# Softmax of later batches transposed by VectorE blocks and a quarter exchange, one TensorE burst per head pair, W_in in 256-column pieces, a new order

## The chip, the cores and the metric

The kernel runs on one core of a Trainium2 chip. The time is that of one execution on the device, in microseconds (us); several runs are taken and their median is given. One further execution was recorded by the hardware profiler, and all rows below are from it.

## What is computed

Eight batches of eight heads, 576 positions, head size 64. The first four heads attend to a local window of 32 positions, the other four to all earlier positions with the same remainder modulo 32. The result, 4608 tokens by 512, goes through a two-layer network with a gate.

```python
scores = scale * np.matmul(q, k.transpose(0, 1, 3, 2))
mask_local = (rel >= 0) & (rel < stride)
mask_strided = (rel >= 0) & (pos[None, :] % stride == pos[:, None] % stride)
...
attn = np.exp(scores - max) / (sum + 1e-09)
x = np.matmul(attn, v)                      # (4608, 512)
h = x @ w_in                                # 512 -> 2048
g = h * erf(softplus(h))
out = g @ w_out                             # 2048 -> 512
```

The weights arrive as 64-bit floats and everything else as 32-bit floats.

## The kernel before

**Precision.** The large products are computed in three terms: each operand is split into a rounded high part and a remainder (`hi`, `lo`), and hi*hi, hi*lo and lo*hi are added up. The 64-bit weights are loaded as pairs of 32-bit words, and VectorE puts a 32-bit float together from their bits (`bits0`, `bits1`, `bits2`, lines 612, 619 and 625), ScalarE takes the high part (line 630), VectorE the remainder (line 633). There are 16 such pieces: eight of W_in (256 rows by 512 columns) and eight of W_out (256 rows by 512 columns), 1 MB each as they are loaded.

**Attention.** `heads` treats one pair of heads of one batch, 32 pairs in all. For masks as sparse as these only small blocks of the scores are computed, 32 or 64 queries by 64 keys, and stacked on the partitions. The steps: load q and k, then v (lines 363, 366); `scores` on TensorE (line 377, 80 small matmuls for a local pair, 48 for a strided one); on VectorE `mask`, `maxi`, `less` (lines 407, 413, 425); `exp` on ScalarE (line 434); `total` and `invert` on VectorE (458, 467, 468); `norm` on GpSimd (475); `turn` on TensorE, six transposes of 128 by 128 into PSUM (484); `fetch`, a copy to SBUF by ScalarE (490); `av` on TensorE (503, 72 or 44 small matmuls); and the split of the result into `xhi` and `xlo` (522, 527). The eight pairs of batches 0 and 1 use other banks and buffers (`PAIRS`); their softmax is partly done by ScalarE alone (449), their mask is added by TensorE (390), and some of their loads lie in buffers that later hold weights. The 24 later pairs use one region `ps` of two PSUM banks, first for the scores, then for the transposed weights of attention, then for the result.

**The network.** A chunk is 512 tokens of a batch; the last 64 tokens of each batch are put by in DRAM (808) and form a ninth chunk of 512 (814). `ftile` treats 128 of the 2048 hidden columns of one chunk, 144 times in all, numbered k: 12 matmuls `mm1` into a bank `h` (line 661, 4 blocks by 3 terms), `softplus` on ScalarE from `h` (666), `gate` (erf, 669), `prod` on VectorE (672, reads `h` again), the two parts `ghi` (675, ScalarE) and `glo` (678, VectorE), and four groups of three matmuls `mm2` into the banks `o0` to `o3` (708). After the last hidden column of a segment the four banks are copied out (729, 727) and stored (732) or added to what is stored (742). Two consecutive ftiles share their activation tables: softplus twice, erf twice. `SEGS` is the order in which chunks 0 and 1 take hidden columns, in segments of 4 or 8 of the 16 blocks, since W_in and W_out are still arriving; chunks 2 to 8 take all 16 at once.

**Order.** `Plan` holds every step with its engine, a duration and a key, and writes down one fixed order for each engine before the kernel is built: at each moment the step with the lowest key among those that could start. `KP`, `KW`, `KI` and `FT` are the keys. Instructions then run on each engine in this order and wait only for semaphores. PSUM has eight banks: `h` two, `ps` two, `o0` to `o3` one each. While TensorE has nothing else in the first stage, `warm` matmuls on constants are put in (851).

Of the kernel before, what the change touches and what calls it, by code (L numbers as in the profile page):

```python
# [31 lines left out]
FT = (150.531, 835.645, -384.189, -1053.44, -681.063, 898.966)  # L32
KI = -3209.9
KW = (
    (101.599, 202.151, -535.174, 604.781, 1212.9, 836.522, 1608.98, 546.558),
    (361.736, 4.05449, 627.481, 738.31, 1066.48, 1640.11, 660.969, 255.795),
)
KP = (
    (95.8804, -1256.4, 246.738, 210.68, 388.629, 267.383, -232.968),
    (89.0881, -257.397, 181.554, 106.998, -422.473, 270.564, -29.6347),  # L40
    (39.7309, 257.811, 444.048, 228.671, -192.767, 289.834, -736.755),
    (-746.766, -31.9878, 336.097, -221.418, 982.13, -1173.26, 113.144),
    (96.5419, -322.814, 849.876, 940.658, 220.734, 127.612, 110.26),
    (448.329, 235.899, 647.027, -140.7, -533.241, 575.841, -534.673),
    (140.403, 484.365, 38.2845, 536.795, -628.605, -59.6376, 5.88654),
    (427.907, 538.096, 156.093, -147.993, -594.918, -613.259, -1.35456),
    (1021.68, 1227.51, 317.55, 1305, 395.946, 827.8, 422.359),
    (-428.223, -259.323, 505.653, -625.444, -366.792, -81.8236, -265.431),
    (22.7174, 1266.92, 869.655, 629.419, 756.918, 1001.81, 769.097),
    (-341.314, 324.887, 467.314, -208.725, 85.0777, -457.75, 85.4845),  # L50
    (-189.06, 539.726, -625.551, -295.899, -556.918, -965.588, -631.652),
    (1609.6, 847.563, 528.29, 890.427, 1474.46, 704.536, 355.295),
    (-514.483, -397.182, -437.853, 681.903, 612.634, 326.529, 1144.86),
    (741.667, 393.174, -749.662, -494.021, 28.442, 173.094, 247.963),
    (797.248, 187.08, 566.957, 523.594, 793.895, 602, 318.908),
    (366.017, -645.078, -99.5954, 310.3, -964.063, 384.338, 209.526),
    (631.465, 206.076, 1156.93, 1362.17, 893.28, 848.748, -88.8396),
    (-200.429, 877.969, 95.2955, 98.2614, 1284.23, 712.113, 133.908),
    (865.298, 648.717, -139.025, 1057.54, 185.411, 1166.19, 1050.68),
    (-66.958, 514.588, 431.303, -298.053, -587.459, 262.919, -968.247),  # L60
    (105.453, -1317.06, 482.08, 483.418, -205.564, -296.236, -661.863),
    (1415.29, 716.979, 102.743, 957.286, 84.2946, 1206.16, 1404.15),
    (1204.17, 47.6775, 1285.08, 758.243, -236.785, 669.252, -244.839),
    (-287.567, 175.767, 268.123, -323.218, 115.933, 679.178, 789.502),
    (-327.873, -43.1518, -1732.87, 33.6649, -446.861, -524.272, -602.082),
    (-670.311, -507.154, -210.895, -8.09243, -684.736, -520.511, 98.5742),
    (-227.431, 682.135, -134.022, 852.457, 1270.14, 204.678, -591.776),
    (652.572, 1156.05, 362.832, 536.18, 486.522, 728.767, 1501.49),
    (-788.051, -1054, -428.762, 166.209, -409, 26.2244, -1458.41),
    (324.91, -145.801, -16.3735, 507.041, -294.342, -261.974, -486.826),  # L70
)
PAIRS = (
    (("h", "h"), None, True, True),
# [8 lines left out]
SEGS = ((0, 0, 4), (1, 0, 4), (0, 4, 8), (1, 4, 8), (0, 8, 16), (1, 8, 16))  # L82
# [5 lines left out]
WQ = max(WL, WS)  # L88
# [3 lines left out]
NCON = 5 * 64 + 64 + P  # L92
# [39 lines left out]
TWO = {"split_lo", "norm", "bits0", "bits1", "bits2", "split_lo_w"}  # L132


class Op:
    def __init__(self, eng, dur, key, emit, after, new, use, earliest):
        self.eng, self.dur, self.key, self.emit, self.earliest = eng, dur, key, emit, earliest
        self.after, self.new = list(after), list(new)
        self.start = self.end = None
        self.tail, self.words, self.table = 0.0, 0, None  # L140
        self.locks = eng == "pool" or eng == "dve" and emit.__name__ in TWO
        for b in self.new + list(use):
            b.users.append(self)


class Plan:
# [7 lines left out]
    PATIENCE = 0.002  # L154
# [35 lines left out]
    def order(self):  # L190
# [5 lines left out]
        while left:  # L196
            best = None
            for e in self.ENGINES:
# [13 lines left out]
                if can:  # L212
                    soon = min(can)[0] + self.PATIENCE
# [23 lines left out]
            if e == "sp":  # L237
                free[e] = t + 0.6
                dma = max(dma, t + 0.6) + o.dur
# [21 lines left out]
def attention_moe(  # L261
# [3 lines left out]
    qk_str: bass.AP,  # L265
    v_loc: bass.AP,
# [21 lines left out]
    ident = cpool.tile([P, P], F32, name="ident")  # L288
# [4 lines left out]
    ident_b = con[:, 384:]  # L293
# [7 lines left out]
    def buf(pool, tag, shape, name, dtype=F32):  # L301
        def make():
            return pools[pool].tile(shape, dtype, tag=tag, name=name, bufs=bufs[tag])

        return Buf(tag, make)

# [11 lines left out]
    def heads(b, hp, keys, ring, before=(), pe_mask=False, pool_norm=True, act_sum=False, banks=None, home=None, own=False):  # L318
# [15 lines left out]
        def region(tags, name):  # L334
            if tags is None:
                return [buf("ps_a", "ps", [P, 2, 512], f"{name}_{pid}")]
            return [buf("ps_h" if t == "h" else "ps_o", t, [P, 512], f"{name}{h}_{pid}") for h, t in enumerate(tags)]
# [141 lines left out]
        def turn(i):  # L479
            def run():  # L480
                for h in range(parts[i].start, parts[i].stop):
                    for w in range(3):
                        c = 64 * (2 * w if 2 * w + 2 <= units else units - 2)
                        yield nc.tensor.transpose(bank(t, h)[:, 128 * w : 128 * w + 128], sm[:, h, c : c + 128], ident)  # L484
# [57 lines left out]
        for i, p in enumerate(parts):  # L542
# [23 lines left out]
            o = add("pe", 0.33 * (p.stop - p.start) + 0.05, k_t + e, turn(i), [o, o_ident] + first[2:3], [y] if not own else [], [sm, y])  # L566
# [22 lines left out]
    def weight(i, src, rows, sl, key):  # L589

        n = 2 * SW
        wide = src.dtype != F32
# [6 lines left out]
        def load():  # L599
            if wide:  # L600
                yield nc.sync.dma_start(
                    words.tile.rearrange("p (c n) t -> p c (n t)", c=2),
                    src.bitcast(U32)[rows, 2 * sl.start : 2 * sl.stop].rearrange("(c p) n -> p c n", c=2),
                )
            else:
                yield nc.sync.dma_start(
                    w.tile.rearrange("p (c n) -> p c n", c=2), src[rows, sl].rearrange("(c p) n -> p c n", c=2)
# [28 lines left out]
        if wide:  # L636
            op = add("sp", P * 8 * n / 3.9e5, key - 8.0, load, new=[words])
# [4 lines left out]
        else:  # L642
            op = add("sp", P * 4 * n / 3.9e5, key - 8.0, load, new=[w])
# [5 lines left out]
    def ftile(k, c, f, first_f, last_f, ready):  # L649

        v0 = PRO + SLOT * k
        ph = buf("ps_h", "h", [P, 512], f"h_{k}")
        a = buf("mpool", "a", [P, CH], f"a_{k}")
        ghi = buf("mpool", "ghi", [P, CH], f"ghi_{k}", F32R)
        glo = buf("mpool", "glo", [P, CH], f"glo_{k}", F32R)

        def mm1():
            c0, fs, s = c % 2 * S, slice(f * P % SW, f * P % SW + P), f * P // SW
# [12 lines left out]
        def prod():  # L671
            yield nc.vector.tensor_tensor(out=a.tile, in0=a.tile, in1=ph.tile, op=ALU.mult)  # L672
# [15 lines left out]
        o = add("act", tp, at(0), softplus, [first] + gates[-1:] * (k % 2 == 0), [a], [ph])  # L688
# [6 lines left out]
        o = add("dve", td, at(2), prod, [o], [], [a, ph])  # L695
# [71 lines left out]
    def load_ident():  # L767
        yield nc.sync.dma_start(ident, ident_f)
# [8 lines left out]
    o_ident = plan.add("sp", 0.2, KI, load_ident)  # L777
# [9 lines left out]
    for f in range(0, DF, SW):  # L787
        for c in range(0, NCC, 2):
            i = len(w1)
            op, pair = weight(i, w_in, slice(c * P, (c + 2) * P), slice(f, f + SW), KW[0][i])  # L790
            w1.append(op)
            win.append(pair)
    for i in range(NFC // 2):
        op, pair = weight(8 + i, w_out, slice(2 * i * P, (2 * i + 2) * P), slice(0, DM), KW[1][i])
# [10 lines left out]
    def stash(b, hp, part, x, done):  # L805
# [4 lines left out]
        return plan.add("sp", 0.1, KP[4 * b + hp][6] + (1.0 + 0.1 * part), run, done)  # L810
# [10 lines left out]
    for b in range(B):  # L821
        p2 = b // 2
        for i, hp in enumerate((0, 1, 2, 3)):
            keys = KP[4 * b + i]
            if p2 == 0:
# [4 lines left out]
                last_av.append(o)  # L830
                for f in home or ():
                    w_load[f].after += loads
            else:
                done, _, _, _ = heads(b, hp, keys, [mm1_of[b - 2], *put[b - 2]], last_av)
            x_of.setdefault(b, []).extend(done)
            put.setdefault(b, []).extend(stash(b, hp, n, x, done) for n, x in enumerate((xhi, xlo)))
# [28 lines left out]
def _layout(q, k, v):  # L865
# [14 lines left out]
    qk_str = np.zeros((B, 2, P, WS), f32)  # L880
# [12 lines left out]
    qk_str[..., :S] = pairs_t(resid(q[:, hl:]))  # L893
    qk_str[..., S + 32 : S + 32 + S] = pairs_t(resid(k[:, hl:]))
# [6 lines left out]
    return qk_loc, qk_str, v_loc.reshape(B, 2, P, VL), v_str.reshape(B, 2, P, VS)  # L901


def _consts():
# [13 lines left out]
    c[:, 384:] = np.eye(P)  # L918
# [34 lines left out]
```

## Time and profile before

| | |
|---|---|
| median of three runs | 925.93 us (924.52 to 926.8) |
| the profiled execution | 924.2 us, of which the span of the trace is 922.4 us |
| mean granted TensorE clock | 0.992 |
| TensorE matmuls, busy | 899.6 us |
| VectorE, busy | 392.4 us |
| ScalarE, busy | 600.8 us |
| GpSimd, busy | 68.8 us |

Busy times are sums over one engine. Matmuls are pipelined, so the time from one matmul to the next is read from the chain that ended last, which counts each moment once, and not from the duration of one matmul.

### The profile page before, as it was taken

What the parts mean: (1) busy time and instruction counts of PE and PEld (TensorE: products, weight loads), DVE (VectorE), ACT (ScalarE), POOL (GpSimd) and SP (SyncE); (2) the same over time, 40 slices, a digit from 0 to 9 for tenths busy, and PEclk for the clock granted to TensorE, in tenths of its full rate; (3) what the DMA queues carried; (4) which work ended last, traced back from release to release, by engine and by line L of the source; (5) the groups of instructions that cost most, each with busy time, mean ns of one, the idle gap of its engine ahead of it and who ended that gap; (6) DMA issues with size and microseconds to landing.
All of it is one profiled execution on the core that took longest, in us unless ns stands there. A gap on an engine that the chain in (4) does not pass through costs nothing.

```text
span 922.4 us, 17778 instructions
## 1 busy us (share of the span) xinstructions
PE 899.6 (98%) x7583; PEld 732.9 (79%) x7588; DVE 392.4 (43%) x617; ACT 600.8 (65%) x906; POOL 68.8 (7%) x68
## 2 busy tenths in 40 slices
PE   5889999999999999999999999999999999999997
PEld 3668888888888888888888888888888888888886
DVE  6899952344444334444433234443344222222222
ACT  4887876667676667666666557575676565556652
POOL 1220011011110000000000001000000100000000
PEclk9799999999999999999999999999999999999999
DMA  9997023314251113111221031111220310001001
GB/s 355 332 350 241 35 43 46 86 48 93 71 113 48 51 39 122 48 59 55 64 79 31 1 104 60 48 63 48 100 69 4 91 47 1 1 0 46 1 1 46
DMA packets 31791, 72.38 MB, mean 78 GB/s; under 512 B 11552, under 2 KB 11808, under 8 KB 31712
## 3 DMA queue, kind: packets, MB, share of 16 engines
q1 hardware_dynamic: 27920, 64.30, 20.4%
q0 software_dynamic: 3552, 6.56, 4.1%
q8 instruction: 59, 0.97, 0.4%
q10 hardware_dynamic: 240, 0.39, 0.1%
q14 instruction: 20, 0.16, 0.1%
HBM read 55.51 MB, written 15.73 MB: 77 GB/s over the span
## 4 chain that ended last, share of the span: by engine, by line
PE 93%; DVE 4%; DMA 1%; issue 1%; ACT 0%; SPq 0%; ACTq 0%
PE o L708 43%; PE h L661 42%; PE x L503 3%; PE s L377 3%; PE t L484 2%; PE s L503 1%; DMA words<-w_in 1%; DVE pair L633 1%; DVE w L625 1%; DVE mx L413 1%; DVE w L619 1%; DMA con<-consts 0%; ACT sm L449 0%; PE s L484 0%; DVE xlo L527 0%
## 5 line engine op out<-in xcount | busy, mean ns | idle before, releaser
L708 PE MATMUL o<-pair,ghi 128*128 128x512 f32 x1152 | 362.2, 396 | 1.9 <-DVE xlo L527 1.9
L661 PE MATMUL h<-xhi,pair 128*128 128x512 f32 x1152 | 288.6, 393 | 0.5 <-DVE a L672 0.5
L661 PEld LDWEIGHTS h<-xhi,pair 128*128 128x128 f32 x1152 | 215.0, 188 | 46.6 <-DVE a L672 1.1
L708 PEld LDWEIGHTS o<-pair,ghi 128*128 128x128 f32 x1152 | 212.3, 188 | 45.6 <-DVE xlo L527 2.0
L708 PE MATMUL o<-pair,glo 128*128 128x512 f32 x576 | 225.0, 391 | 0.0
L666 ACT ACTIVATE a<-h 128x512 f32<-128x512 f32 x144 | 85.9, 598 | 182.6 <-PE h L661 182.1
L678 DVE TENSOR_TENSOR glo<-a,ghi 128x512 fp32r<-128x512 f32 x144 | 98.4, 692 | 177.3 <-ACT ghi L675 171.1
L672 DVE TENSOR_TENSOR a<-a,h 128x512 f32<-128x512 f32 x144 | 93.6, 682 | 160.3 <-ACT a L669 160.3
L661 PE MATMUL h<-xlo,pair 128*128 128x512 f32 x576 | 154.1, 389 | 0.0
L708 PEld LDWEIGHTS o<-pair,glo 128*128 128x128 f32 x576 | 108.4, 188 | 23.2
L661 PEld LDWEIGHTS h<-xlo,pair 128*128 128x128 f32 x576 | 108.1, 188 | 22.7
L675 ACT CAST ghi<-a 128x512 fp32r<-128x512 f32 x144 | 88.9, 621 | 39.1 <-PE o L708 25.2
L666 ACT ACT_TABLE_LOAD x73 | 93.7, 1283 | 3.7 <-PE h L661 2.4
L669 ACT ACT_TABLE_LOAD x72 | 92.4, 1283 | 1.3
L669 ACT ACTIVATE a<-a 128x512 f32<-128x512 f32 x144 | 84.3, 626 | 0.8
L475 POOL TENSOR_TENSOR sm<-sm,r 128x768 f32<-128x768 f32 (+2 forms) x27 | 37.6, 1391 | 522.4 <-DVE r L468 418.8
L527 DVE TENSOR_TENSOR xlo<-x,xhi 128x256 fp32r<-128x256 f32 (+3 forms) x48 | 19.7, 451 | 63.2 <-ACT xhi L522 63.1
L458 DVE TENSOR_REDUCE r<-sm 128x12 f32<-128x768 f32 (+1 forms) x25 | 22.2, 889 | 54.5 <-ACT sm L434 54.5
L407 DVE TENSOR_TENSOR s<-s,con 128x640 f32<-128x640 f32 (+1 forms) x24 | 21.5, 897 | 44.8 <-PE s L377 44.8
L377 PEld LDWEIGHTS s<-qk 64*32 64x32 f32 (+1 forms) x2048 | 28.2, 120 | 11.8 <-issue 8.9
L729 ACT COPY ob<-o 128x512 f32<-128x512 f32 x50 | 28.8, 588 | 11.5 <-PE o L708 8.5
L490 ACT COPY sm<-t 128x768 f32<-128x768 f32 x24 | 19.2, 798 | 24.3 <-PE t L484 23.9
(55 smaller groups left out, 487.6 us busy)
## 6 DMA issues: line engine op xcount, KB each, us to landing
v<-v_loc SPq DMA_DIRECT2D x16, 640.0 KB, 4.0
qk<-qk_str SPq DMA_DIRECT2D x16, 608.0 KB, 4.1
qk<-qk_loc SPq DMA_DIRECT2D x16, 592.0 KB, 4.5
words<-w_out SPq DMA_DIRECT2D x8, 1024.0 KB, 8.0
words<-w_in SPq DMA_DIRECT2D x8, 1024.0 KB, 7.6
out<-ob SPq DMA_DIRECT2D x32, 256.0 KB, 2.1
v<-v_str SPq DMA_DIRECT2D x16, 384.0 KB, 3.2
out<-ob POOLq DMA_DIRECT2D x16, 256.0 KB, 4.9
```

Source lines behind the costliest of these rows:

```text
L377: yield nc.tensor.matmul(bank(s, h)[m * j : m * (j + 1), 64 * t : 64 * (t + 1)], queries(rows, q0, m), keys_of(rows, q0), start=(h, j) not ...
L458: yield nc.vector.tensor_reduce(out=rc[:, parts[i], :units], in_=wide(sm[:, parts[i]]), axis=mybir.AxisListType.X, op=ALU.add)
L475: yield (nc.gpsimd if pool_norm else nc.vector).tensor_tensor(out=d, in0=d, in1=spread(rc, i), op=ALU.mult)
L503: yield nc.tensor.matmul(bank(px, m)[h * D : (h + 1) * D, a * n : (a + 1) * n], values(rows, (2 * a + h) * D), pt[rows, h, c : c + n], sta ...
L661: yield nc.tensor.matmul(ph[:, :CH], win[2 * s + cc // 2][:, w, fs.start + cc % 2 * SW : fs.stop + cc % 2 * SW], x[cc][:, c0 : c0 + CH], s ...
L666: yield nc.scalar.activation(a.tile, ph.tile, AF.Softplus)
L669: yield nc.scalar.activation(a.tile, a.tile, AF.Erf)
L672: yield nc.vector.tensor_tensor(out=a.tile, in0=a.tile, in1=ph.tile, op=ALU.mult)
L675: yield nc.scalar.copy(ghi.tile, a.tile)
L678: yield nc.vector.tensor_tensor(out=glo.tile, in0=a.tile, in1=ghi.tile.bitcast(F32), op=ALU.subtract)
L708: yield nc.tensor.matmul(po.tile, g[:, ts], wout[f // 2][:, w, f % 2 * SW : f % 2 * SW + SW], start=(f == first_f and i == 0), stop=(f == ...
L729: yield nc.scalar.copy(ob[:, oh], po.tile)
```

## The change

**Later batches.** For batches 2 to 7 `heads` is replaced by a class `Pair` and a function `burst`. The six TensorE transposes and the ScalarE copy behind them are gone. In their place VectorE transposes blocks of 32 by 32 (`flip`, two instructions a pair), GpSimd copies the four quarters that are already on the right 32 partitions (`stay`), and SyncE issues four DMAs from SBUF to SBUF for the quarters that must change partitions (`exchange`). `claim` is a step without an instruction, which reserves the buffer. The scores are stacked in another order so that this gives the layout that `av` wants; the strided pairs get an input of their own with padded queries (`qk_res`, 1312 columns in place of 1216) and a mask of their own.

**One burst.** `av` of one pair and `scores` of the next are one uninterrupted run of matmuls. The pairs of a batch go in the order 0, 2, 1, 3, so that local and strided ones alternate. The results of `av` go to two banks `c` and `h`; `ps` holds scores only.

**PSUM and the late ftiles.** `h` has one bank in place of two, `c` is new. Ftiles with k below 16 alternate between `h` and `c`; from k = 16 on all use `h`, and VectorE first copies `h` to SBUF (`keep`, into `hs`), from where softplus and the product read. Buffers: `a` 3 in place of 4, `ghi` and `glo` 2 in place of 3, `sm` 2 in place of 1.

**Weights.** A piece of W_in is now 512 rows by 256 columns (it was 256 by 512), so the first two blocks of hidden columns need one piece where they needed two. The load of each piece has a key of its own (`KL`). `SEGS` has four segments in place of six. All keys are new (not shown), and the planner waits a little for a step with a lower key on ScalarE and VectorE.

```diff
-SEGS = ((0, 0, 4), (1, 0, 4), (0, 4, 8), (1, 4, 8), (0, 8, 16), (1, 8, 16))
+SEGS = ((0, 0, 4), (1, 0, 6), (0, 4, 16), (1, 6, 16))
+EARLY = 16
+ORDER = (0, 2, 1, 3)
...
-    PATIENCE = 0.002
+    PATIENCE = {"pe": 0.002, "act": 0.3, "dve": 0.2, "pool": 0.002, "sp": 0.002}
...
-    bufs = {"qk": 1, "v": 1, "sm": 1, "mx": 2, "r": 2, "ps": 1, "h": 2, "a": 4, "ghi": 3, "glo": 3,
-            "ob": 2}
+    bufs = {"qk": 1, "v": 1, "sm": 2, "mx": 2, "r": 2, "ps": 1, "h": 1, "c": 1, "hs": 2, "a": 3, "ghi": 2, "glo": 2, "ob": 2}
...
+    class Pair:
...
+        def soft(self):
...
+            def flip():
+                src = sm[:, :, :cols].rearrange("p h (u f q) -> p h u f q", f=2, q=32)
+                flat = tt.tile.rearrange("p h c -> p (h c)")[:, : 2 * cols]
+                for h in range(2):
+                    yield nc.vector.transpose(
+                        flat.rearrange("p (f h u q) -> p h u f q", f=2, h=2, q=32)[:, h], src[:, h]
+                    )
...
+            def stay():
+                for m in range(2):
+                    for f in range(2):
+                        yield nc.gpsimd.tensor_copy(pt[quarter(m, f), f, :], plane(m, f, f))
+
+            def exchange():
+                for m in range(2):
+                    for f in range(2):
+                        yield nc.sync.dma_start(pt[quarter(m, f), 1 - f, :], plane(m, 1 - f, f))
...
+            o = add("pool", 0.1 + n / 500.0, k_n + 0.1, norm, [o], [], [sm, rc])
+            o = o_t = add("dve", dve(n) + 0.07, k_t, flip, [o, *turn_of("t")], [tt], [sm])
+            o = add("pool", 0.0, k_t + 0.1, claim, [o], [pt])
+            self.ready = [
+                add("pool", 4 * (0.06 + cols / 1000.0), k_t + 0.2, stay, [o], [], [tt, pt]),
+                add("sp", 1.0, k_t + 0.2, exchange, [o], [], [tt, pt]),
+            ]
...
+    def burst(p, n, ring=(), before=()):
...
+        if p:
+            p.x = [buf("ps_h", "ch"[m], [P, 512], f"x{m}_{p.pid}") for m in range(2)]
+            after += [*p.ready, p.lv, *ring]
...
+        if n:
+            n.s = buf("ps_a", "ps", [P, 2, 512], f"s_{n.pid}")
+            after += [n.lq, *o_con]
...
+        def run():
+            if p:
+                yield from p.av()
+            if n:
+                yield from n.scores()
...
     def ftile(k, c, f, first_f, last_f, ready):
...
-        ph = buf("ps_h", "h", [P, 512], f"h_{k}")
+        early = k < EARLY
+        ph = buf("ps_h", "hc"[k % 2 if early else 0], [P, 512], f"h_{k}")
...
+        hs = ph if early else buf("mpool", "hs", [P, CH], f"hs_{k}")
...
-                    ph[:, :CH], win[2 * s + cc // 2][:, w, fs.start + cc % 2 * SW : fs.stop + cc % 2 * SW], x[cc][:, c0 : c0 + CH], start=(i == 0), stop=(i == len(terms) - 1)
+                    ph[:, :CH], win[f // 2][:, w, 2 * P * cc + f0 : 2 * P * cc + f0 + P], x[cc][:, c0 : c0 + CH], start=(i == 0), stop=(i == len(terms) - 1)
...
+        def keep():
+            yield nc.vector.tensor_copy(hs.tile, ph.tile)
+
         def softplus():
-            yield nc.scalar.activation(a.tile, ph.tile, AF.Softplus)
+            yield nc.scalar.activation(a.tile, hs.tile, AF.Softplus)
...
-            yield nc.vector.tensor_tensor(out=a.tile, in0=a.tile, in1=ph.tile, op=ALU.mult)
+            yield nc.vector.tensor_tensor(out=a.tile, in0=a.tile, in1=hs.tile, op=ALU.mult)
...
-    for f in range(0, DF, SW):
-        for c in range(0, NCC, 2):
-            i = len(w1)
-            op, pair = weight(i, w_in, slice(c * P, (c + 2) * P), slice(f, f + SW), KW[0][i])
...
+    for i in range(NFC // 2):
+        op, pair = weight(i, w_in, slice(0, DM), slice(2 * i * P, 2 * (i + 1) * P), KW[0][i], KL[0][i])
...
-            ready = (x_of[c] + w1[2 * (f // 4) : 2 * (f // 4) + 2], [w2[f // 2]])
+            ready = (x_of[c] + [w1[f // 2]], [w2[f // 2]])
```

## Rows read from the trace of the kernel before

**Rows 1.** The five stages: each engine's busy us (instructions), granted clock, DMA.

```profile
6.00:39.00 33.00, 25.99 (x636) 18.70 (x640) 26.93 (x58) 23.28 (x108) 8.74 (x9) 0.88 0.98 370
39.00:75.00 36.00, 31.93 (x498) 25.21 (x499) 34.26 (x52) 27.12 (x56) 6.55 (x4) 0.92 0.96 347
75.00:917.00 842.00, 841.70 (x6451) 689.02 (x6450) 330.79 (x509) 548.92 (x740) 53.21 (x50) 1.00 0.19 54
917.00:922.40 5.40, 0.00 (x0) 0.00 (x0) 0.42 (x1) 0.00 (x0) 0.00 (x0) 0.93 0.62 182
```

**Rows 2.** The chain that ended last, 75.22 to 916.7 us, shares by line.

```profile
by line: PE o L708 46.8%; PE h L661 45.7%; PE x L503 3.0%; PE s L377 2.6%; PE t L484 1.9%
```

**Rows 3.** Pieces of that chain in order of time: start us, us, what.

```profile
219.12 0.86 PE s L377 x48
...
233.83 0.66 PE t L484 x6
234.48 1.39 PE o L708 x6
235.87 0.84 PE x L503 x44
236.71 2.27 PE o L708 x9
238.97 0.97 PE s L377 x64
239.94 5.71 PE h L661 x24
...
253.13 1.30 PE x L503 x72
...
264.05 5.44 PE h L661 x24
```

**Rows 4.** Groups of instructions by form: count, busy us, mean ns of one, idle before.

```profile
L484 PE MATMUL t<-ident,sm 128*128 128x128 f32 x144 | 19.6, 272 | 0.0
...
L727 DVE COPY ob<-o 128x512 f32<-128x512 f32 x2 | 1.4, 690 | 6.3 <-PE o L708 6.3
...
L425 DVE TENSOR_TENSOR sm<-s,mx 128x768 f32<-128x768 f32 x13 | 12.4, 954 | 0.7
...
L475 POOL TENSOR_TENSOR v<-v,r 128x384 f32<-128x384 f32 x4 | 3.3, 828 | 17.9 <-DVE r L468 12.7 <-ACT xhi L522 4.8 <-ACT pair L630 0.4
...
L490 ACT COPY sm<-t 128x768 f32<-128x768 f32 x24 | 19.2, 798 | 24.3 <-PE t L484 23.9
```

**Rows 5.** DMA: issue to landing of the small stores; instruction fetch.

```profile
q8 instruction: 59, 0.97, 0.4%
...
rests<-xhi SPq DMA_DIRECT2D x32, 32.0 KB, 3.1
```

**Rows 6.** TensorE in order of time, 46 to 50 us: start us, us.

```profile
46.13 0.91 PE L503 MATMUL s<-qk,v 64*64 64x54 f32 x44
46.97 1.04 PE L377 MATMUL s<-qk 64*32 64x64 f32 x80
47.93 0.45 PE L390 MATMUL s<-con 128*128 128x320 bf16 x2
48.22 0.82 PE L484 MATMUL s<-ident,sm 128*128 128x128 f32 x6
```

**Rows 7.** The first `mm1` and the weight piece ahead of it, in order of time.

```profile
38.52 1.23 DVE L633 TENSOR_TENSOR pair<-w,pair 128x1024 fp32r<-128x1024 f32 x1 [1.32 <-ACT pair L630]
...
39.77 2.79 PE L661 MATMUL h<-xhi,pair 128*128 128x512 f32 x8
```

**Rows 8.** Matmuls of `mm1` and `mm2` from 0 to 75 us, TensorE and weight loads.

```profile
0.00:75.00 75.00, 12.16 (x48) 9.57 (x49) 0.91 0.94 346
...
0.00:75.00 75.00, 9.09 (x30) 6.00 (x30) 0.91 0.94 346
```

More of the change, by code (lines that the diff above doesn't have):

```diff
@@ L237, in order @@
             if e == "sp":
-                free[e] = t + 0.6
-                dma = max(dma, t + 0.6) + o.dur
+                free[e] = t + 0.6 * o.issues
+                dma = max(dma, t + 0.6 * o.issues) + o.dur
                 o.end = dma + 2.0
@@ L565, in heads @@
             y = t[i] if len(t) > 1 else t[0]
-            o = add("pe", 0.33 * (p.stop - p.start) + 0.05, k_t + e, turn(i), [o, o_ident] + first[2:3], [y] if not own else [], [sm, y])
+            o = add("pe", 0.33 * (p.stop - p.start) + 0.05, k_t + e, turn(i), [o, o_ident] + first[2:3], [y] if not own else [], [sm, y, ident])
             first.append(o)
@@ new lines, in turn_of, with split_hi, split_lo_x @@
+    def turn_of(name):
+        return [turns[name]] if name in turns else []
+    def burst(p, n, ring=(), before=()):
+        after, new, use, dur, words, key = [*turn_of("b"), *before], [], [], 0.36, 0, 0.0
+        if p:
+            p.x = [buf("ps_h", "ch"[m], [P, 512], f"x{m}_{p.pid}") for m in range(2)]
+            after += [*p.ready, p.lv, *ring]
+            new += p.x
+            use += [p.v, p.pt]
+            dur += 1.15 if p.loc else 0.69
+            words += 144 if p.loc else 88
+            key = p.keys[6]
+        if n:
+            n.s = buf("ps_a", "ps", [P, 2, 512], f"s_{n.pid}")
+            new.append(n.s)
+            after += [n.lq, *o_con]
+            use.append(n.qk)
+            dur += 0.82 if n.loc else 0.71
+            words += 160 if n.loc else 96
+            key = n.keys[2]
+        def run():
[3 more added lines that the diff above has]
+                yield from n.scores()
+        o = plan.add("pe", dur, key, named("burst", run), after, new, use)
+        o.words = words
+        turns["b"] = o
+        if n:
+            n.o_s = o
+        done = []
+        if p:
+            for m, z in enumerate(p.x):
+                def split_hi(m=m):
+                    src, hi = p.views(m, xhi[p.hp])
+                    yield nc.scalar.copy(hi, src)
+                def split_lo_x(m=m):
+                    src, hi = p.views(m, xhi[p.hp].bitcast(F32))
+                    _, lo = p.views(m, xlo[p.hp])
+                    yield nc.vector.tensor_tensor(out=lo, in0=src, in1=hi, op=ALU.subtract)
+                w = (320 if m else 256) if p.loc else (252 if m else 324)
+                o = plan.add("act", act(w, 0.06), p.keys[6] + (0.1 + 0.01 * m), split_hi, [o if m == 0 else turns["b"]], [], [z])
+                done.append(plan.add("dve", dve(w), p.keys[6] + (0.2 + 0.01 * m), split_lo_x, [o], [], [z]))
+        return done
@@ L591, in weight @@
+    def weight(i, src, rows, sl, key, k_l):
         n = 2 * SW
+        blocks = (rows.stop - rows.start) // P
         wide = src.dtype != F32
@@ L687, in ftile @@
         first.words = 24
-        o = add("act", tp, at(0), softplus, [first] + gates[-1:] * (k % 2 == 0), [a], [ph])
+        o = first
+        if not early:
+            o = add("dve", td, at(2), keep, [o], [hs], [ph])
+        o = add("act", tp, at(0), softplus, [o] + gates[-1:] * (k % 2 == 0), [a], [hs])
         o.table = "softplus"
@@ L808, in run, with finish @@
             yield nc.sync.dma_start(rests[hp, part, :, b * REST : (b + 1) * REST], x[hp][:, c0 : c0 + REST].bitcast(F32))
-        return plan.add("sp", 0.1, KP[4 * b + hp][6] + (1.0 + 0.1 * part), run, done)
+        return plan.add("sp", 0.1, KP[4 * b + (hp if b < 2 else ORDER.index(hp))][6] + (1.0 + 0.1 * part), run, done)
+    def finish(b, hp, done):
+        x_of.setdefault(b, []).extend(done)
+        put.setdefault(b, []).extend(stash(b, hp, n, x, done) for n, x in enumerate((xhi, xlo)))
     def reload(hp, part, x, after):
@@ L822, in attention_moe @@
         p2 = b // 2
-        for i, hp in enumerate((0, 1, 2, 3)):
+        for i, hp in enumerate(ORDER if p2 else (0, 1, 2, 3)):
             keys = KP[4 * b + i]
@@ L830, in attention_moe @@
                 last_av.append(o)
+                if home is None:
+                    turns["q"], turns["v"] = loads
                 for f in home or ():
                     w_load[f].after += loads
[L833 to L836, printed above, removed]
+                finish(b, hp, done)
+            elif i == 0 and b == 2:
+                pair = Pair(b, hp, keys)
+                pair.loads()
+                burst(None, pair, before=last_av)
+                pair.soft()
+            if p2:
+                n = 4 * b + i + 1
+                follow = Pair(n // 4, ORDER[n % 4], KP[n]) if n < 4 * B else None
+                if follow:
+                    follow.loads()
+                finish(b, pair.hp, burst(pair, follow, [mm1_of[b - 2], *put[b - 2]]))
+                if follow:
+                    follow.soft()
+                pair = follow
         if b == 1:
```

265 lines of the change are left out of this document (200 added, 65 removed).

## Prediction

> **What bounds the kernel now.** I read first the busy time by stage. From 75 to 917 us TensorE is busy 841.7 of 842 us, at a granted clock of 1.00, while VectorE is busy 330.8, ScalarE 548.9 and GpSimd 53.2 us [rows 1]. A busy TensorE is not one at its peak, so the second view is the chain that ended last over the same stretch: 46.8 + 45.7 = 92.5% are the large matmuls, 7.5% the attention, and no wait has a share [rows 2]. A run of 24 `mm1` matmuls takes 5.44 us, 0.2267 us each [rows 3]. By 75 us 48 + 30 of the 3456 large ones are done [rows 8], so 3378 are left: 765.7 us of the 841.5 us of the chain. The remaining 76 us are 24 head pairs, 3.2 us each, and only they can shrink in this stage.
>
> Before 75 us another thing binds. Between 6 and 39 us TensorE is busy 26.0 of 33 us at a clock of 0.88, and between 39 and 75 us 31.9 of 36 us at 0.92, while VectorE is busy 26.9 and 34.3 us and the DMA engines have shares of 0.98 and 0.96 [rows 1]. VectorE builds weights there and does the softmax of eight pairs; it and the transfers set when `x` of batches 0 and 1 is ready. The last 5.4 us are the last copy and store.
>
> **The later pairs on TensorE.** The six transposes of a pair hold the chain for 0.66 us [rows 3]; 144 of them are 24 visits [rows 4], 24 x 0.66 = 15.8 us, and 1.9% of 841.5 us [rows 2] is 16.0, the same. After them six `mm2` take 1.39 us in place of 6 x 0.2267 = 1.36: 0.03 a visit, 0.7 us. After `av` nine `mm2` take 2.27 in place of 2.04 us, and after `scores` 24 `mm1` take 5.71 in place of 5.44 [rows 3]: coming back to the large matmuls costs 0.23 to 0.27 us. With `av` and the next `scores` in one run this is paid once a pair and not twice: 24 x 0.23 = 5.5 us. The small matmuls keep their number and sizes. Together 15.8 + 0.7 + 5.5 = 22.0 us leave TensorE. The bounds are 16.5 (merging saves nothing) and 16.5 + 24 x 0.27 = 23.0.
>
> **A long run of small instructions.** The burst has 44 + 80 or 72 + 48 matmuls, 240 to 248 instructions with their weight loads. Instruction fetch comes in packets of 0.97 MB / 59 = 16 KB [rows 5]. At 46.13 us 44 + 80 + 2 + 6 matmuls, 264 instructions, ran in 2.9 us with no idle time between them [rows 6], as dense as the burst. I cost it at nothing. The upper bound is one packet that comes late by its whole time: 0.4% of 16 engines' 922.4 us over 59 packets [rows 5] is 1.0 us, at each of 24 bursts 24 us, which would undo the gain; the dense run just named speaks for the lower end.
>
> **The chain of a pair.** In place of transposes and `fetch` (0.66 and 0.80 us [rows 3, 4]) come `flip`, `stay`, `exchange`. The trace shows no VectorE transpose; the nearest row is a pass over the same 768 columns, 0.95 us [rows 4]. I take 1.0 us for the two instructions, between 0.9 and 2 (two slower passes). `stay` is four GpSimd copies of up to 384 columns; a product of that width takes 0.83 us [rows 4], so at most 3.3 us, and less for one operand. `exchange` is four DMAs of some 40 KB; the 32 KB stores to `rests` land 3.1 us after issue [rows 5], so about 4.3 us with four issues. Today the `scores` that end at 219.98 lead to the transposes at 233.83 us, 13.9 us later [rows 3]. With flip and exchange `av` would follow about 13.9 + 1.0 + 4.3 = 19.2 us after `scores`. A later batch has 16 ftiles of 5.44 us and four bursts of about 2.2 us, 96 us or 24 us a pair: covered by 5 us. It is tightest at batch 2, whose `av` must wait for the last `mm1` of chunk 0 (now k = 21) and be done before k = 32: three more pairs need 3 x 21.4 = 64 us and TensorE has 10 x 5.44 + 8.8 = 63 us plus the `mm2` that are behind. Cost taken 0, up to 5 us. Behind `exchange` on SyncE's queue stand the loads of the next pair and the stores, whose buffers have been free for long; behind `stay` on GpSimd only the next `norm`.
>
> **One bank for the late ftiles.** 128 ftiles now free `h` by a copy. The only such copy here, 128x512 from PSUM by VectorE, takes 0.69 us [rows 4]; with its hand-over about 0.8 us (estimate). VectorE gets 128 x 0.69 = 88 us and 24 x 1.0 us more: 331 + 112 = 443 of about 820 us, 54%, not the bound. But today at least 54 times in this stage two ftiles' `mm1` run back to back as 24 matmuls, as at 239.94 and 264.05 us [rows 3], which needs two banks. What must cover the copy is two groups of `mm2`, 6 x 0.2267 = 1.36 us, put between the two `mm1`. There are four groups an ftile, so such an order exists; if it is kept the cost is 0, if pairs stay back to back it is up to 64 x 0.8 = 51 us. The value I take is 2 us in all, nearest to the rows of a TensorE that never waits. ScalarE loses 24 x 0.80 us of `fetch` and becomes no bound either.
>
> The Trainium skill (Perfetto Trace Analysis, section Matmuls) speaks against this part: independent groups of matmuls should rotate through several PSUM banks, so that emptying one overlaps the matmuls of the next. By that rule the late ftiles would pay the copy each time, and the sum would be the second rival's.
>
> **The start.** The first `mm1` at 39.77 us began 0.02 us after a weight piece was ready [rows 7], and it needs two pieces of W_in; now it needs one. The last of the steps that VectorE does for a piece is 1.23 us [rows 7]; there are four. At most 7.0 + 4.1 us of idle TensorE and (0.12 x 26 + 0.08 x 32) = 5.7 us of lower clock could come back [rows 1]: 17 us. Against it stand fewer buffers for `a`, `ghi` and `glo` just when VectorE is full, up to 5 us. I take 3 us gained, about two of those steps, since the second piece may come later and the loads may go in another order; range -5 to +10. The fewer copies to `ob` (two segments less) are on ScalarE, under TensorE's matmuls: nothing. The end is the same.
>
> **Sum.** From the profiled execution's 924.2: -22 -3 +2 = 901.2. The median of the runs shown is 1.7 us higher; I forecast the median, 902.5 us.
>
> **The rivals.**
> First, part of the gain goes into new waits: `h` not empty in a third of the 64 pairs (21 x 0.8 = 17 us less what two groups cover, say 8), or batch 2 late by 5 us. Time 906 to 917. For it: new steps with durations the trace doesn't show. Against it: TensorE waits nowhere after 75 us now. Chance 0.18.
> Second, the other side: the single bank decides. The `mm1` of an ftile waits for `keep` behind VectorE's other work. At 0.2 us for each of the 128 late ftiles the 25 us are gone; with 64 exposed copies of 0.8 us the time is 902 + 51 = 953. For it: at least 54 back-to-back pairs now. Against it: the `mm2` groups that can be put between, and VectorE at 54%. Chance 0.09.
> Third, the start gains much more than 3 us, because VectorE and the transfers are given work in the order of need: 902 - 8 to - 14, so 888 to 894. Chance 0.10.
> Fourth, gains and losses cancel, 923 to 929, for instance by bursts that each wait 1 us for `exchange`: 0.03.
> The forecast, 894 to 906, has 0.60.
>
> **How the numbers follow.** Faster is the forecast, the third rival and nearly all of the first: 0.87; no change 0.04; slower 0.09. A difference of 0.3% (2.8 us) is about what a measurement of this kernel can tell from none. The range, 888 to 917, holds the forecast, the first rival and most of the third, and leaves out 0.16 or so for the second, the fourth and the ends.
>
> **What would show it.** Right: no transposes by TensorE after batch 1; x and s pieces adjacent in the chain, one return of about 0.25 us behind each; still no wait from 80 us to the end; `keep` at about 0.69 us; runs of 12 `mm1` with `mm2` between them from k = 16 on. The stage after the first steady matmul should be 20 us shorter, the rest at the start. Wrong: `mm1` that wait for `keep` on VectorE, bursts that wait for SyncE's DMA or GpSimd, a granted clock below 1.00 after 80 us, or steady work that begins later than 75 us.

## The result and the profile after

The changed kernel takes 910.22 us (median of 4 runs, 909.77 to 910.73) against 925.22 us for the kernel before beside it: a ratio of 0.9837, 95% interval 0.9819 to 0.9854. It is faster, as forecast, and inside the range; the forecast of 902.5 us is 7.7 us too low, where the gain itself is 15.0. The profiled execution took 910.45 us with a span of 908.7.

Busy time by stage of the kernel after, the columns as in [rows 1]:

```profile
6.00:39.00 33.00, 18.73 (x520) 13.84 (x515) 25.59 (x47) 17.22 (x78) 7.19 (x7) 0.84 1.00 384
39.00:75.00 36.00, 27.14 (x531) 21.52 (x524) 34.76 (x57) 29.37 (x79) 6.60 (x6) 0.92 0.93 338
75.00:903.30 828.30, 828.11 (x6383) 682.54 (x6381) 439.14 (x690) 540.42 (x722) 102.01 (x138) 1.00 0.19 58
```

Against [rows 1] the long stage is as full as before and ends 13.4 us earlier (903.3, not 916.7), with VectorE up by 108 us. But the two stages ahead of it are emptier: TensorE does 18.7 us of work from 6 to 39 us where it did 26.0, and 27.1 us from 39 to 75 where it did 31.9, with VectorE and the transfers about as busy as they were. Of the 12.1 us that are missing, 4.5 are `warm` matmuls, which only fill in: there were 15 of them (5.1 us), and there is one now (0.6 us). The first `mm1` comes 7.9 us later than in [rows 7]:

```profile
47.62 2.15 PE L900 MATMUL h<-xhi,pair 128*128 128x512 f32 x8
```

The chain that ended last, its shares by line from 84.48 us on, answers to [rows 2]:

```profile
by line: PE o L953 47.3%; PE h L900 46.3%; PE x L669 3.0%; PE s L649 2.5%; DVE hs L905 0.2%; ACT L908 0.2%; ACT L911 0.2%; issue 0.1%; DVE a L914 0.1%; ACT a L911 0.1%; ACT a L908 0.1%; ACTq L908 0.0%
```

The transposes (1.9% before) are gone. Pieces of that chain, start us and us, answer to [rows 3]:

```profile
305.82 2.72 PE h L900 x12
308.54 1.36 PE o L953 x6
309.90 1.12 PE x L669 x66
...
311.19 0.73 PE s L649 x42
311.93 6.35 PE o L953 x27
...
335.28 0.84 PE x L669 x44
336.11 0.97 PE s L649 x64
337.08 3.62 PE o L953 x15
```

From k = 16 on the `mm1` of an ftile are a run of 12, 2.72 us, with at least two groups of `mm2` (1.36 us) ahead of the next. `av` and the next `scores` stand together, and one return follows them: 15 `mm2` take 3.62 us in place of 15 x 0.2267 = 3.40. The new steps, with their mean ns, and the one wait of TensorE from 84 us to the end (total us, times, longest):

```profile
L905 DVE COPY hs<-h 128x512 f32<-128x512 f32 x128 | 88.0, 688 | 158.6 <-PE h L900 158.6
...
L748 POOL COPY pt<-tt 32x384 f32<-32x384 f32 x48 | 28.0, 583 | 19.2 <-DVE tt L732 17.5
...
L732 DVE STREAM_TRANSPOSE tt<-sm 128x384 f32<-128x384 f32 x24 | 12.4, 554 | 7.0 <-POOL sm L726 7.0
```

```profile
pt<-tt SPq DMA_DIRECT2D x48, 48.0 KB, 1.9
```

```profile
PE h L900 <- DVE hs L905: 0.2, 1, 0.2
```

**Where the 13.4 us come from.** Before, the steady stage ran from 75.22 to 916.7 us with 78 large matmuls done: 765.7 us for the rest of them and 75.8 us for the pairs. After, from 84.48 us with 72 done to 903.3: 818.8 us, of which 3384 x 0.2267 = 767.1 are large matmuls, and 51.7 us are left; with the first later `scores` (0.97 us, just ahead of it) 52.7. The pairs shrank by 23.1 us. The start: steady work begins at 83.52 with 6 fewer large matmuls done (1.4 us), so at 84.9 where it was 75.2, a loss of 9.7 us. -23.1 + 9.7 = -13.4. The steady part did what was forecast; the start did the opposite. Part of the loss is the granted clock: from 75 to 85 us TensorE is busy all the time in both kernels, at 1.00 before and at 0.78 after, which is about 2 us of work (an estimate, 10 x 0.22).

### The profile page after: what moved, and what is told of

The parts are those of the page before. It is cut to its first block, busy times and chain, and to the rows that moved or that the text cites. A ratio compares the mean times of both kernels' runs of the same rounds, so it can differ in the third digit from the quotient of the medians.

```text
span 908.7 us, 18092 instructions
## 1 busy us (share of the span) xinstructions
PE 874.5 (96%) x7425; PEld 718.4 (79%) x7427; DVE 500.2 (55%) x793; ACT 588.5 (65%) x880; POOL 116.1 (13%) x156
## 4 chain that ended last, share of the span: by engine, by line
PE 92%; DVE 4%; ACT 2%; DMA 1%; issue 1%; SPq 0%; POOL 0%; DVEq 0%; ACTq 0%; POOLq 0%
PE o L953 44%; PE h L900 42%; PE x L669 3%; PE s L649 2%; ACT v L470 1%; DMA con<-consts 1%; DVE pair L870 1%; PE s L524 0%; DVE mx L434 0%; DVE w L856 0%; DVE w L862 0%; DVE w L849 0%; PE s L505 0%; DVE xlo L548 0%; DVE a L914 0%
## 5 line engine op out<-in xcount | busy, mean ns | idle before, releaser
L953 PEld LDWEIGHTS o<-pair,ghi 128*128 128x128 f32 x1152 | 215.2, 189 | 48.1 <-DVE xlo L548 2.7
L905 DVE COPY hs<-h 128x512 f32<-128x512 f32 x128 | 88.0, 688 | 158.6 <-PE h L900 158.6
L908 ACT ACTIVATE a<-hs 128x512 f32<-128x512 f32 x128 | 80.9, 632 | 99.1 <-DVE hs L905 84.7
L914 DVE TENSOR_TENSOR a<-a,hs 128x512 f32<-128x512 f32 x128 | 85.3, 708 | 102.1 <-ACT a L911 102.0
L726 POOL TENSOR_TENSOR sm<-sm,r 128x640 f32<-128x640 f32 (+1 forms) x24 | 36.3, 1513 | 470.3 <-DVE r L723 451.8
L748 POOL COPY pt<-tt 32x320 f32<-32x320 f32 (+1 forms) x96 | 53.1, 553 | 39.5 <-DVE tt L732 36.0
L974 ACT COPY ob<-o 128x512 f32<-128x512 f32 x42 | 24.2, 585 | 10.9 <-PE o L953 8.6
L669 PEld LDWEIGHTS x<-pt,v 64*64 64x64 f32 x1392 | 24.4, 134 | 8.5 <-issue 8.5
```

Source lines behind the costliest of these rows:

```text
L669: yield nc.tensor.matmul(self.x[m][d, n * a : n * (a + 1)], self.v[rows, (2 * a + h) * D : (2 * a + h) * D + D], p, start=True, stop=True,)
L726: yield nc.gpsimd.tensor_tensor(out=wide(sm), in0=wide(sm), in1=spread(rc), op=ALU.mult)
L748: yield nc.gpsimd.tensor_copy(pt[quarter(m, f), f, :], plane(m, f, f))
L905: yield nc.vector.tensor_copy(hs.tile, ph.tile)
L908: yield nc.scalar.activation(a.tile, hs.tile, AF.Softplus)
L914: yield nc.vector.tensor_tensor(out=a.tile, in0=a.tile, in1=hs.tile, op=ALU.mult)
```

## The experiments

The theory at first: the start lost time because the constants, on which the mask of the first scores waits, are now the seventh load on SyncE and not the third; they landed at 12.38 us, and VectorE's first softmax step moved from 8.83 to 13.44 us. The rival: something else in the start's order is later still. Unless it is said otherwise, an experiment is made from the changed kernel.

**The constants first.**

```diff
+    ops = plan.order()
+    ops.remove(o_con[0])
+    ops.insert(0, o_con[0])
-    for op in plan.order():
+    for op in ops:
```

> The changed kernel with one transfer moved: the constants are the first load on SyncE's queue in place of the seventh; every other order is as it was. First theory (the late constants hold the start back): the first mask on TensorE runs at 6 to 8 us in place of 12.4, VectorE's first softmax step at about 9 us in place of 13.4 to 15.8, x of batch 0 is ready at 38 to 40 us (45.1 before), and the time falls by 5 to 7 us, to 903 to 905. Rival (VectorE's weights and the transfers as a whole bind the start, the constants only come first in a queue of waits): x of batch 0 gains under 2 us, and the time is 908 to 910.

911.98 us (909.94 to 913.71, ratio 0.9867, interval 0.9849 to 0.9884): no gain. The constants landed early (the first mask ran on TensorE at 7.35 us, not at 12.43), and the chain shows what came next, start us and us:

```profile
2.13 6.37 DMA words<-w_out
...
8.53 0.70 DVE w L849
...
12.85 1.23 DVE pair L870
14.08 0.88 DVE mx L434
```

VectorE's order has the first W_out piece ahead of the first softmax step. The theory falls for the changed kernel.

**The kernel before with its constants seventh**, the other loads as they were.

```diff
+    lead = [o for o in [o for o in ops if o.eng == "sp"][:7] if o is not o_con[0]] + [o_con[0]]
+    for o in lead:
+        ops.remove(o)
+    ops[0:0] = lead
```

> The kernel before with the opposite edit: the constants are its seventh load in place of the third. First theory: VectorE's first softmax step moves from 8.8 us to about 15 us, and the time rises by 5 to 7 us, to 930 to 932. Rival (the start is bound elsewhere): under 2 us, 925 to 927.

930.71 us against 924.05 (ratio 1.0072, 1.0058 to 1.0086): 6.7 us lost. The same place costs in one order and is hidden in the other.

**The first W_out piece behind the first softmax.** Constants first, and that piece's load just ahead of the first W_in load, its five steps ahead of the third piece's.

```diff
+    for o in [loads[0], *piece]:
+        ops.remove(o)
+    i = ops.index(third)
+    ops[i:i] = piece
+    ops.insert(ops.index(loads[1]), loads[0])
```

> The changed kernel with its first piece of work put in another order: the constants are the first load; the first W_out piece is loaded later, just ahead of the first W_in piece, and its five steps on VectorE and ScalarE stand ahead of the third piece instead of ahead of all softmax steps. Theory (the start is lost because VectorE's first softmax steps stand behind a weight piece and behind late transfers): VectorE's first softmax step at about 8 us (13.4 before, 14.1 with the constants alone moved), x of batch 0 ready at 38 to 41 us (45.1), time 903 to 906. Rival (what binds the start is the sum of ScalarE's and VectorE's work up to then, whatever comes first): x of batch 0 gains under 2 us, time 908 to 911.

915.21 us (914.86 to 915.79, ratio 0.9909), 5 us worse. The softmax began at 7.94 us, 5.5 us sooner, but little of that lasted. The next transfer in the row, a q and k load, was 11.97 us on its way, so that the scores of the fourth pair ran at 19.42 us (21.35 in the changed kernel). Those of the fifth pair then stood 3.03 us idle and were no sooner than in the changed kernel (26.93). And the five steps of the piece that was moved now stand ahead of the split of a later result, on VectorE and, with one step, on ScalarE. In order of time, TensorE and VectorE:

```profile
27.43 1.40 PE L398 MATMUL s<-qk 64*32 64x64 f32 x80 [3.03 <-issue]
...
42.59 0.59 PE L1111 MATMUL warm<-con 128*128 128x512 bf16 x1 [4.63 <-DVE xlo L548]
43.53 2.36 PE L524 MATMUL s<-sm,v 64*64 64x32 f32 x72 [0.36 <-issue]
```

```profile
26.52 0.82 DVE L548 TENSOR_TENSOR xlo<-s,xhi 128x324 fp32r<-128x324 f32 x2
...
34.58 1.06 DVE L849 TENSOR_SCALAR w<-words 128x1024 uint32<-128x1024 uint32 x1
...
39.77 1.23 DVE L870 TENSOR_TENSOR pair<-w,pair 128x1024 fp32r<-128x1024 f32 x1 [1.11 <-ACT pair L867]
...
42.12 0.42 DVE L548 TENSOR_TENSOR xlo<-s,xhi 128x256 fp32r<-128x256 f32 x1
```

The same two steps, `xlo` and the `av` behind it, in the changed kernel:

```profile
36.41 0.41 DVE L548 TENSOR_TENSOR xlo<-s,xhi 128x256 fp32r<-128x256 f32 x1
...
38.36 1.37 PE L524 MATMUL s<-sm,v 64*64 64x32 f32 x72 [0.36 <-ACT sm L511]
```

Up to 37 us this kernel is 0.4 us behind the changed one (the last transposes at 37.12 and 36.73 us); that `av` is 5.2 us behind, and the time is 5.0 longer. So what the early softmax had gained was gone by the fifth pair, and the moved piece then cost its time in the new place. TensorE's granted clock up to 85 us was 0.74 here, 0.88 in the changed kernel.

The profile has no releaser for the 3.03 us. The times give one: the scores start 0.09 us after the `xlo` steps end (26.52 + 0.82 = 27.34). In the changed kernel it is 26.01 + 0.82 = 26.83 and 26.93, with constants first 26.24 + 0.82 = 27.06 and 27.16, and in the changed kernel TensorE's sequencer stood 2.18 us in a semaphore wait at that line. So I read it as a bank that `xlo` frees. It is not what the changed kernel lost: these scores are those of the first pair of batch 1, and in the kernel before they ran later still, at 58.08 us.

**Only the loads in the order of before.** The other engines keep their order; `planned` is the changed kernel's order and `ops` that of the next experiment, whose loads stand as in the kernel before.

```diff
+    loads = [o for o in ops if o.emit.__name__.startswith("load") and id(o) in head]
+    into = {id(o): x for o, x in zip([o for o in planned if o in loads], loads)}
+    queues["sp"] = [into.get(id(o), o) for o in planned if o.eng == "sp"]
```

> The changed kernel with only its loads in the order in which the kernel before issues them (constants third, first W_in piece eighth, and so on); TensorE, VectorE, ScalarE and GpSimd keep the changed kernel's order. If the order of the loads is what costs the start: x of batch 0 near 38 to 40 and total 902 to 905. If it is the order on the computing engines (VectorE's first W_out piece ahead of the first softmax, the pairs' order): within 3 us of 910, or above it where a load that the compute order wants early now lands late.

939.03 us (938.8 to 941.38, ratio 1.0164): 29 us worse than the changed kernel, with a granted clock of 0.73 up to 85 us. The chain now begins with two transfers that the old order of the other engines wants late and the new one early:

```profile
4.29 11.43 DMA words<-w_in
...
15.73 13.30 DMA v<-v_str
```

**The whole start in the order of before.** The loads, the 16 weight pieces, the eight pairs of batches 0 and 1 and the first eight ftiles are 359 steps in both kernels, one for one. They take the places that they have in the changed kernel's order, but in the sequence of the kernel before, with its fill-in matmuls.

```diff
+    names = [(x if isinstance(x, str) else plan_ops[x]) for x in SEQ]
...
+    for o in planned:
+        if id(o) in head:
...
+            wanted.append(names.pop(0))
+        elif not (o.eng == "pe" and o.emit.__name__ == "run"):
+            wanted.append(o)
```

> The changed kernel, but its first 359 steps (the loads, the weight pieces, the eight pairs of batches 0 and 1, and the first eight ftiles) and the fill-in matmuls stand in the order in which the kernel before has them; the rest keeps its own order. First theory (the 9.7 us that the start lost come from the order of the start alone): first softmax step on VectorE near 8.8 us, x of batch 0 near 37 to 39, first mm1 near 40 to 41 (before 39.8, after 47.6), the first later scores some 7 to 9 us earlier than at 83.5, total 901 to 904. Rival (the start is held by the parts of the change itself: the new weight pieces, the bank that is split over h and c, fewer steps left to cover with): first mm1 not before 45, total 908 to 912.

916.39 us (913.12 to 917.14, ratio 0.9907, 0.989 to 0.9923). The first `mm1` came at 39.99 us, as in the kernel before, and the total became worse. Busy time by stage of this kernel, then TensorE's wait from 78 us on:

```profile
75.00:85.00 10.00, 10.00 (x121) 8.06 (x120) 9.10 (x12) 4.18 (x6) 0.00 (x0) 1.00 0.79 260
85.00:100.00 15.00, 11.86 (x46) 9.30 (x45) 10.65 (x16) 13.17 (x18) 1.57 (x2) 0.89 0.23 88
```

```profile
PE h L901 <- DVE a L915: 7.4, 5, 3.1
```

Either VectorE cannot carry an early start together with the new work, or this is only the seam between two orders: weight steps stand ahead of the products that free `h`. The next run tells these apart.

**The start first, the rest planned round it.** The 319 of those steps that the kernel before's plan starts in its first 90 us get the lowest keys, in its sequence; the kernel's own planner orders everything else anew.

```diff
+    for i, t in LEAD.items():
+        plan.ops[i].key = t - 1e6
     for op in plan.order():
```

> The changed kernel, but those of the first 359 steps that the kernel before's plan starts in its first 90 us come first in its order wherever they are ready; everything else is ordered anew round them by the kernel's own planner (e9 had kept the changed kernel's order for the rest). First theory (the start's loss is one of order, and what e9 lost behind 85 us was the seam between two orders, where VectorE's weight steps stood ahead of products that free bank h): first mm1 near 40 us, first later scores 78 to 82 us, no wait of TensorE over 1 us behind 85 us, total 901 to 905. Rival (VectorE, with the later pairs' steps and the copies of h on top of the weights, cannot carry the early start): waits of TensorE for VectorE's products between 85 and 140 us as in e9, total 908 to 916.

902.67 us (901.87 to 905.03) against 924.77, ratio 0.9766, interval 0.9745 to 0.9787, which lies below that of the changed kernel: this version beats both. The first `mm1` came at 40.30 us. One expectation missed: the first later scores came at 85.44 us, not at 78 to 82, because the plan puts large matmuls ahead of them. The better measure is how many of the 3456 large matmuls are done (the sum of the instructions of `mm1` and `mm2` in the windows from 0):

| by us | before | after | old sequence in the new places | start first, rest planned |
|---|---|---|---|---|
| 85 | 117 | 75 | 116 | 119 |
| 150 | 400 | 361 | 349 | 397 |
| 200 | 598 | 563 | 551 | 598 |

`mm1` and `mm2` by 85 us (count in the first bracket, then the granted clock behind the second), of the kernel before and of the changed one:

```profile
0.00:85.00 85.00, 17.79 (x72) 13.91 (x72) 0.92 0.93 337
...
0.00:85.00 85.00, 12.73 (x45) 8.73 (x45) 0.92 0.93 337
```

```profile
0.00:85.00 85.00, 13.82 (x51) 10.43 (x52) 0.88 0.89 330
...
0.00:85.00 85.00, 8.62 (x24) 5.87 (x24) 0.88 0.89 330
```

The same of this version, by 85 and 200 us, `mm1` and then `mm2`, and its TensorE wait from 78 to 400 us:

```profile
0.00:85.00 85.00, 17.65 (x72) 13.88 (x72) 0.92 0.91 330
...
0.00:200.00 200.00, 77.94 (x324) 60.88 (x324) 0.97 0.51 173
```

```profile
0.00:85.00 85.00, 13.07 (x47) 9.24 (x48) 0.92 0.91 330
...
0.00:200.00 200.00, 67.80 (x274) 51.77 (x275) 0.97 0.51 173
```

```profile
PE h L901 <- DVE hs L906: 0.2, 1, 0.2
```

At 200 us it is 35 large matmuls, 7.9 us, ahead of the changed kernel; its span is 6.7 us shorter (902.0 and 908.7). So VectorE can carry the early start, and the loss was one of order. With the order two other things came back that no run takes apart from it: 9 `warm` matmuls in place of one, and a granted clock of 0.92 up to 85 us in place of 0.88.

The stage behind hides none of this. From the first matmul of the later scores to the last large matmul, with 0.2267 us added for each large one done ahead of it, the changed kernel takes 836.2 us, with constants first 836.2, with the start reordered 836.2, with the loads alone as before 836.1; the kernel before takes 859.2 and this version 838.4. So the first four differ in the start alone, and this version gains in the start alone.

**The steady part: the kernel before without the later pairs' transposes.** Their 144 transposes are left out; ScalarE's copy stays, of the weights that are not transposed.

```diff
         def turn(i):
             def run():
+                if not own:
+                    return
```

> The kernel before, with the six transposes of each of the 24 later pairs left out (ScalarE copies the untransposed weights of attention onto themselves, so the output isn't the reference's); order and waits as they were. Theory (the transposes stand in full on the path that sets the end): 24 x 0.69 = 16.5 us less, about 907.5. Rival (TensorE would have waited there anyway): under 5 us less.

908.67 against 923.96 us (ratio 0.9842, 0.9826 to 0.9858): 15.3 us, with 16.5 forecast for them. In the profiled execution the stage behind the first later scores is 14.2 us shorter (845.0 us in the measure above, for 859.2). They stood on the path nearly in full.

**The burst broken by one group of `mm2`** between `av` and `scores`, in all 23 bursts that have both.

```diff
             if p:
                 yield from p.av()
-            if n:
-                yield from n.scores()
```

> The changed kernel with one step of TensorE's order (a group of large matmuls) put between av and the next scores, 23 times: two returns to the large matmuls per pair again. First theory (a return costs 0.23 to 0.27 us): 5.3 to 6.2 us more, 915.5 to 916.5. Rival (the joined run saves nothing, or pays it back in instruction fetch): within 1 us of 910.2.

927.0 us (926.14 to 928.08, ratio 1.0029, 1.0018 to 1.0039), 16.8 above the changed kernel and not the 5 to 6 expected. The extra return is what it should be, and something else came with it. From the chain of this kernel:

```profile
655.04 0.87 DVE mx L709
...
656.00 0.13 DVE sm L712
...
656.88 0.32 DVE xlo L818
...
657.21 0.49 DVE xlo L818
...
657.84 3.00 PE h L901 x12
...
675.80 0.84 PE x L669 x44
676.63 0.89 PE o L954 x3
677.53 0.97 PE s L649 x64
678.50 2.94 PE o L954 x12
```

Three `mm2` behind `av` take 0.89 us in place of 0.68, 0.21 for the return. In the 11 bursts that begin with a strided pair that is all. In the 12 that begin with a local pair it is 0.35 us (3.06 us from the first `av` matmul to the large ones behind `scores`, 0.68 of it `mm2`, where the joined run takes 2.03). Together that is 6.5 us. Then `mm1` wait for bank `h`, which holds half of the result of `av`: it comes free with the last `xlo`, which now stands behind the next pair's softmax on VectorE. This kernel's waits from 80 us on (total us, times, longest):

```profile
PE h L901 <- DVE xlo L818: 4.1, 14, 0.7
```

14 waits of 4.1 us in all, and behind them runs of about 3.0 in place of 2.72 us, 14 x 0.29 = 4.1: with the 6.5 that is 14.7 of the 16.8 us. Another 0.9 is the start, which the edit does not touch (the first matmul of the later scores at 84.30 us, not at 83.45). About 1 us I can't place.

**The copy of `h` doubled.**

```diff
             yield nc.vector.tensor_copy(hs.tile, ph.tile)
+            yield nc.vector.tensor_copy(hs.tile, ph.tile)
```

> The changed kernel with the copy of h done twice for each of the 128 late ftiles, 77 us more for VectorE. Theory (the two mm2 groups cover 1.36 us, of which copy and hand-over need 0.8): the doubled copy needs about 1.4 us, so 0 to 0.15 us at 64 places, up to 10 us more, 910 to 920. Rival (the cover is used up already, or VectorE is near its bound): 0.6 us at 64 places, 38 us more, about 948.

965.64 us in one run, 55 us more, beyond what was expected with or without cover. 3 us of it were lost in the start, which the edit does not touch (the first matmul of the later scores at 86.50 us, the clock 0.78 up to 85 us). The other 52 are 0.41 us for each of 128 extra copies of 0.69 us: two groups of `mm2` cover one copy and not two. TensorE's `mm1` (count, busy us, mean ns, idle before and its releasers):

```profile
L900 PE MATMUL h<-xhi,pair 128*128 128x512 f32 x1152 | 302.2, 405 | 17.9 <-DVE hs L906 12.8
```

**Two ftiles' `mm1` back to back again**, at 49 places, the two groups of `mm2` behind the second.

```diff
+    j = ops.index(kp) + 1
+    ops[j:j] = [m1, *early]
```

> The changed kernel with the two mm2 groups between two mm1 moved behind the second mm1, at 49 places from k = 16 on, so that nothing covers the copy of the one bank. First theory (a copy of 0.69 us with its hand-over is paid in full where nothing covers it): 49 x 0.8 = 39 us more, about 949. Rival (the copy is mostly hidden otherwise, 0.2 us a place or less): under 920.

1011.97 us in one run, 101.5 us of span more, 2.1 us at each place and not the 0.8 of a bare copy. A place in its chain:

```profile
846.10 0.70 DVE hs L905
...
846.84 3.04 PE h L900 x12
...
849.89 0.70 DVE hs L905
...
850.64 3.04 PE h L900 x12
```

The second `mm1` waits 0.78 us for the copy, and each run then takes 3.04 us, 0.32 more than 2.72. The rest is a second wait, 1.67 us ahead of the first `mm1` here, for a copy that stands behind ScalarE and VectorE's product of the ftile before. This place costs 0.78 + 1.67 + 2 x 0.32 = 3.1 us; 2.1 is the mean of all 49.

## Why the prediction was right, and where not

- **Later pairs off TensorE: right.** -22.0 forecast, -23.1 measured, just past the bound of 23.0. The transposes alone gave 15.3 in the run without them, and splitting the bursts cost 6.5, where 5.5 was taken for joining them: the term that was a little small is probably that one.
- **A long burst and the chain of a pair: right that they cost TensorE nothing.** The weight loads of the 24 bursts start 0.35 us late each (8.5 us in all), and no matmul waits for it. `flip` took 0.89 to 1.04 us a pair (1.0 taken), `stay` 1.9 to 3.3 us (at most 3.3), and each transfer of `exchange` landed 1.9 us after its issue (3.1 taken).
- **One bank: right in the sum, wrong in the margin.** The 2 us for new stalls were 0.2. The copy took 0.69 us as read. But the forecast priced a lost cover at 0.8 us, and the runs show 2.1 us; and the doubled copy, one of 0.69 us, cost 0.41 of them. The place of `av` and `scores` matters for the same bank. The Trainium skill (Perfetto Trace Analysis, section Matmuls) says to rotate banks so that emptying one overlaps the next group. The runs agree with it only where the order gives no other cover, 2.1 us at each of 49 places; with `mm2` in between, one bank cost 0.2 us in all.
- **The start: the step that failed.** "I take 3 us gained", range -5 to +10 gained; it lost 9.7 us. The step weighed the parts of the change (one weight piece in place of two) and put the new order down as an uncertainty. The order was the larger thing: with the old sequence of the start and a plan round it the same parts give 902.67 us, while moving one load, or one piece, or all loads alone gave nothing or less. By 85 us the changed kernel is 42 large matmuls behind, 9.5 us, and nothing later can bring them back, since the stage behind is full. The forecast had named this sign of being wrong, steady work later than 75 us; it came, and so did a lower clock in the start (0.88 up to 85 us, 0.92 before), where part of 5.7 us was to come back. The gain of 3 us from the single weight piece was seen nowhere: with the old sequence the first `mm1` came at 40.30 us (39.77 before [rows 7]), and 119 large matmuls were done at 85 us in place of 117.
- The start missed by 12.7 us, the rest came 3.1 us better than taken (-23.1 with its stalls, for -22 + 2). The direction is right because the gain of the steady part is the larger one, and that was sized well. That the time lies inside the range is in part luck: 910 us is where the first rival stood (906 to 917), and its cause, new waits behind 75 us, did not come. How the 9.7 us are shared out among the single positions of the start's order, the `warm` matmuls and the clock stays open; no run changed one alone with the rest planned round it.

## What to carry to other kernels

A stage in which the bounding engine never waits gives back nearly all that is taken from it (23.1 us for 22.0 here, 15.3 for 16.5 in the run without transposes). A start bound by several engines at once does not follow from its parts: a new order is a change of its own, and it is priced by counting the bounding engine's work done by a given time, before and after. A position in an order (a load, a piece) had no price of its own here: it cost nothing, 5 or 7 us by what stood round it. The whole sequence on all engines is what is to be compared.

## What was unexpected

- Idle time marked "issue" can be a wait for a bank: 1.26, 1.23 and 3.03 us, each ended 0.09 to 0.10 us after the VectorE steps that, as I read it, free it.
- Lost cover cost more than the copy behind it, 2.1 us where the copy is 0.69, since the copy itself then waits its turn among the other steps of VectorE.
- Coming back from the small matmuls cost 0.21 us after `av` even when only three large ones follow; coming back from a wait of 0.78 us cost 0.32.
- A 48 KB exchange between SBUF tiles landed in 1.9 us, sooner than the 32 KB stores to DRAM of [rows 5].
